# Sign of the weights by a rectifier's slope, and a weight decode laid over two steps, in an attention block with two MLPs

## The chip, the cores and the metric

The kernel runs on one core of one Trainium2 chip. The metric is the device time of one execution in microseconds; the time before is the median of three runs. A core has a matrix engine (TensorE; PE in the profile, with PEld for its loads of the stationary operand), a vector engine (VectorE; DVE), a scalar engine (ScalarE; ACT), a general engine (GpSimd; POOL) and a queue engine (SyncE; SP). Each works through its own list of instructions in order; semaphores hold an instruction until its inputs are there and its output buffer is free.

## The reference

```python
scores = softmax over states of x @ state^T / 8      # x: 8 batches, 8 heads, 512 x 64; state: 32 x 64
xread  = a @ state                                    # 8, 8, 512, 64
sread  = softmax over tokens of state @ x^T / 8, @ x  # 8, 8, 32, 64
x = concatenate(xread, sread), heads put side by side # 4352 tokens x 512

h = x @ w_in                                          # 512 -> 2048
x = (h * (1.0 / (1.0 + np.exp(-1.702 * h)))) @ w_out  # 2048 -> 512, first MLP
h = x @ w_in2
out = (h * np.cos(h)) @ w_out2                        # second MLP
```

The four weight matrices arrive as 64-bit floats, everything else as 32-bit floats.

## The kernel before

**Tiles and steps.** The tokens are nine tiles: the 512 read tokens of each batch (tiles 0 to 7) and the 256 state tokens of all batches together (tile 8, the tail). The hidden dimension of 2048 is cut into 16 chunks c of 128. A step is one (MLP m, tile t, chunk c). The first MLP takes its tiles in the order 0 to 6, 8, 7, the second 0 to 3, 8, 4 to 7. In each step TensorE computes `hidden` (the chunk's 128 columns of h into a PSUM tile ph), then `second` for the chunk two steps earlier (LAG = 2), which adds into four PSUM tiles py; ScalarE and VectorE make the activation in between (`gate` in the first MLP, `cosine` in the second). All of it stands in an order written out by hand.

**Two halves.** Each product is made of three matmuls: operands are split into a high half (a ScalarE copy into a rounded type) and a low half (a VectorE subtraction), and high x high, high x low and low x high are added. So a step of a full tile has 12 matmuls of 512 columns in `second`, and 12 in `hidden`, or 6 in tiles 1 to 7 of the first MLP: there the weights are multiplied by the batch's state beforehand (`sw_piece`: six matmuls of 256 columns, a ScalarE copy and a VectorE subtraction into a tile swo, and a write to DRAM from GpSimd's queue), and come back by `load_sw` as swt. The list `sw_steps` says in which step which of 16 pieces for each pair of batches is made. The attention of the next batch is spread over the steps in small parts too (`plan`).

**Decoding.** The 64-bit weights are fetched in units (128 x 1024 words each; 8 units of w_in and 8 of w_out for each MLP, `fetch_w`) and turned into two halves in five passes over 128 x 1024 elements:

- L117, ScalarE: the upper 32-bit word, read as a float and scaled, gives u (the exponent shifted into place);
- L122, ScalarE: the lower word, scaled to its top three bits, in place;
- L125, VectorE: u shifted left by three, OR the three bits;
- L128, VectorE: the sign bit of the upper word, OR u;
- L141, ScalarE: the high half; L143, VectorE: the low half.

L117 and L122 of one unit (`decode_begin`) stand in a step behind ScalarE's split of the gate's product (L367); L125 and L128 stand at that step's very end on VectorE, ahead of the next step's product (L377); L141 and L143 (`decode_end`) stand in the next step. The units of the first MLP are decoded in steps 0 to 13 of tile 0, w_out's and w_in's by turns; a w_out unit j is begun in step 2j and used by `second` in step 2j + 2. Those of the second MLP are decoded in the tail's steps 8, 11 and 14, in the odd steps of tile 7, and in steps 0, 2, 4, 6 and 8 of the second MLP's tile 0 (`at2`).

**Sums.** When a tile's 16 chunks are done, four `store`s copy py to SBUF (ScalarE, L444), and SP's queue writes them out. The copies use two buffers; the first MLP's tiles then come back by `load_y`. The buffers of the state pieces (swo) and of d in `cosine` are two others, with the tag "g".

Of the kernel before, what the change touches and what calls it, by code (L numbers as in the profile page):

```python
# [10 lines left out]
F32 = mybir.dt.float32  # L11
F32R = mybir.dt.float32r
I32 = mybir.dt.int32
U32 = mybir.dt.uint32
# [8 lines left out]
P = 128  # L23
# [18 lines left out]
def attention_two_mlps(  # L42
# [64 lines left out]
    def decode_begin(m, nm, j):  # L107

        raw = rawt.pop((m, nm, j))
        low, high = raw[:, :, 0], raw[:, :, 1]
        u = wtp.tile([P, UNIT], F32, name="u", tag="u")
        ui = u.bitcast(I32)

        nc.scalar.activation(out=u, in_=high.bitcast(F32), func=AF.Copy, scale=2.0**-112)  # L117
        wt[m, nm, j] = u
        begun.append((m, nm, j))

        def act():
            nc.scalar.activation(out=low, in_=low.bitcast(U32), func=AF.Copy, scale=TOP3)  # L122
# [9 lines left out]
        return act, bits  # L132

    def decode_end():

        if not begun:
            return lambda: None
        m, nm, j = begun.pop(0)
        u = wt[m, nm, j]
        w = wp.tile([P, 2, UNIT], F32R, name=f"w{nm}{m}_{j}", tag=f"w{nm}{j}")  # L140
        nc.scalar.activation(out=w[:, 0, :], in_=u, func=AF.Copy)  # L141
        wt[m, nm, j] = (w[:, 0, :], w[:, 1, :])
        return lambda: nc.vector.tensor_tensor(out=w[:, 1, :], in0=u, in1=w[:, 0, :].bitcast(F32), op=ALU.subtract)  # L143
# [227 lines left out]
    def gate(t, c, stores, unit):  # L371

        ph = ht.pop((0, t, c))
# [15 lines left out]

    def cosine(t, c, stores, before, unit, end):  # L390

        ph = ht[1, t, c]
# [4 lines left out]
        low_w = decode_end()  # L397
# [5 lines left out]
        act, bits = decode_begin(*unit) if unit else ((lambda: None),) * 2  # L403
# [4 lines left out]
        act()  # L408
        if low and not end:
            low()  # L410
        low_w()
# [3 lines left out]
        return bits  # L415
# [62 lines left out]
    def warm(n):  # L478
# [25 lines left out]
        ((0, 1), [(0, c) for c in (2, 4, 6, 7, 7, 10, 11, 11, 13, 13, 15)] + [(1, c) for c in (2, 3, 6, 8, 9)]),  # L504
        ((1, 10), [(1, c) for c in range(12, KF)] + [(2, c) for c in (2, 4, 5, 6, 9, 10, 11, 12, 14, 15)] + [(3, 0), (3, 2)]),
        ((3, 3), [(3, c) for c in (6, 9, 10, 12, 14, 15)] + [(4, c) for c in (2, 4, 6, 9, 10, 12, 14, 15)] + [(5, 0), (5, 2)]),
        ((5, 4), [(5, c) for c in (6, 9, 10, 12, 14, 15)] + [(6, c) for c in (2, 4, 5, 6, 9, 10, 11, 12, 14, 15)]),
# [34 lines left out]
    with tc.manual_schedule():  # L542
# [27 lines left out]
        act, bits = decode_begin(0, *seq[0])  # L570
        act()
# [3 lines left out]
        do("xread 0")  # L575
        bits()
        low_w = decode_end()
        do("sum_n 1", "turn_n 1", "split_x 0")
        low_w()
        do("xread 1")  # L580
        load_pair(0)
        act, bits = decode_begin(0, *seq[1])
        act()
        do("split_x 1")
        bits()
# [11 lines left out]
        at2 = [(0, B, c) for c in (8, 11, 14)] + [(0, B - 1, c) for c in range(1, KF, 2)] + [(1, 0, c) for c in range(0, 10, 2)]  # L597
# [98 lines left out]
```

## Time and profile before

| | |
|---|---|
| median of 3 runs | 1528.39 us (1526.99 to 1528.8) |
| profiled execution, its own time | 1530.31 us |
| its span | 1528.5 us |
| mean granted TensorE clock | 0.988 |
| TensorE busy | 1466.0 us (96%) |
| VectorE busy | 966.3 us (63%) |
| ScalarE busy | 644.1 us (42%) |
| GpSimd busy | 110.8 us (7%) |
| first slice of 38 us: TensorE busy | 7 tenths |
| slices 2 to 4: TensorE busy | 8, 7, 8 tenths; VectorE 8, 7, 7 |
| slices 20 and 21 (726 to 802 us): TensorE busy | 8, 8 tenths; VectorE 7, 7 |

Matmuls are pipelined and their ends are modelled, so a busy TensorE is not TensorE at its peak: what counts is how many matmuls start in a stretch. Idle time of an engine that no one waits for costs nothing. PEclk is the clock that the throttle granted, 1.00 or 0.50 of 2.4 GHz.

### The profile page before, as it was taken

Reading aid. Unit: us, or ns where it says so; the run is one execution under the profiler, and the core shown is the slowest. Engines: PE = TensorE matmul, PEld = TensorE weight load, DVE = VectorE, ACT = ScalarE, POOL = GpSimd, SP = SyncE. Lnnn points to the kernel's source line nnn. Section 1 sums busy time; section 2 is a strip of 40 time slices with the busy share of each in tenths; the row PEclk is TensorE's granted clock in tenths of the full one; section 3 lists DMA queues with packets and bytes.
Section 4 is the critical chain, followed back from the end, with each engine's and each line's share of the span. In section 5 each row is a group of like instructions: output and inputs, shape, how many; then the busy total and the mean of one; then the engine's idle time right before and its main releaser. Section 6 shows DMA issues by size and latency. Waiting matters only on the chain.

```text
span 1528.5 us, 19319 instructions
## 1 busy us (share of the span) xinstructions
PE 1466.0 (96%) x7306; PEld 1195.1 (78%) x7306; DVE 966.3 (63%) x1674; ACT 644.1 (42%) x1078; POOL 110.8 (7%) x155
## 2 busy tenths in 40 slices
PE   7878999999999999999889999999999999999998
PEld 4756777778887887897667888888888888888886
DVE  6877565546464646446778666666668666666665
ACT  4555334343434343345565433333344333333433
POOL 0011011110111000100001000010001010101000
PEclk8999999999999999999999999999999999999999
DMA  9544556564556343465320100101010001010000
GB/s 332 177 148 119 167 162 172 156 180 134 165 142 179 109 138 97 113 198 172 110 83 1 49 6 1 56 1 42 1 56 12 31 1 56 1 56 0 28 1 28
DMA packets 81340, 140.58 MB, mean 92 GB/s; under 512 B 11616, under 2 KB 38368, under 8 KB 81248
## 3 DMA queue, kind: packets, MB, share of 16 engines
q1 hardware_dynamic: 72000, 109.60, 22.5%
q0 software_dynamic: 8960, 29.37, 8.0%
q8 instruction: 57, 0.93, 0.3%
q10 hardware_dynamic: 288, 0.39, 0.1%
q14 instruction: 35, 0.29, 0.1%
HBM read 92.14 MB, written 47.19 MB: 91 GB/s over the span
## 4 chain that ended last, share of the span: by engine, by line
PE 74%; DVE 13%; ACT 7%; DMA 3%; issue 3%; SPq 0%; POOL 0%; ACTq 0%; DVEq 0%
PE py L438 38%; PE ph L360 23%; PE ph L353 8%; PE psS L170 2%; DVE u L125 2%; DVE u L128 2%; DVE t L377 1%; DMA yd<-o 1%; ACT u L117 1%; ACT gh L367 1%; PE psC L313 1%; ACT rawo L122 1%; PE psA L229 1%; DVE gl L369 1%; DVE wo L143 1%
## 5 line engine op out<-in xcount | busy, mean ns | idle before, releaser
L360 PE MATMUL ph<-xh,wi 128*128 128x512 f32 (+1 forms) x1280 | 406.2, 381 | 1.5 <-DVE t L377 1.5
L438 PE MATMUL py<-gh,wo 128*128 128x512 f32 (+1 forms) x1152 | 368.2, 382 | 17.0 <-ACT wo L141 9.6
L438 PE MATMUL py<-wo,gh 128*128 128x512 f32 x1088 | 337.6, 391 | 6.0 <-ACT o L444 5.3
L360 PEld LDWEIGHTS ph<-xh,wi 128*128 128x128 f32 x1280 | 238.7, 189 | 51.2 <-DVE t L377 1.9
L438 PEld LDWEIGHTS py<-gh,wo 128*128 128x128 f32 x1152 | 214.8, 190 | 65.6 <-ACT wo L141 12.1
L360 PE MATMUL ph<-xl,wi 128*128 128x512 f32 (+1 forms) x640 | 242.3, 381 | 0.0
L438 PEld LDWEIGHTS py<-wo,gh 128*128 128x128 f32 x1088 | 203.6, 189 | 48.9 <-ACT o L444 6.7
L438 PE MATMUL py<-gl,wo 128*128 128x512 f32 (+1 forms) x576 | 219.2, 381 | 0.0
L438 PE MATMUL py<-wo,gl 128*128 128x512 f32 x544 | 213.5, 392 | 4.8 <-DVE gl L369 4.7
L367 ACT ACTIVATE gh<-t 128x512 fp32r<-128x512 f32 (+1 forms) x144 | 87.6, 608 | 300.8 <-DVE t L377 185.9
L369 DVE TENSOR_TENSOR gl<-t,gh 128x512 fp32r<-128x512 f32 (+1 forms) x144 | 97.5, 677 | 166.7 <-ACT gh L367 166.7
L407 ACT ACTIVATE r<-r,half_pi 128x512 f32<-128x512 f32 (+1 forms) x144 | 101.0, 701 | 239.2 <-DVE r L406 239.2
L400 DVE TENSOR_SCALAR r<-r 128x512 f32<-128x512 f32 (+1 forms) x144 | 64.0, 444 | 176.2 <-ACT r L395 175.5
L353 PE MATMUL ph<-xh,swt 128*128 128x512 f32 x448 | 162.4, 403 | 7.5 <-DVE t L377 5.1
L395 ACT ACTIVATE r<-ph 128x512 f32<-128x512 f32 (+1 forms) x144 | 82.4, 573 | 169.1 <-PE ph L360 168.8
L377 DVE SCALAR_TENSOR_TENSOR t<-t,ph 128x512 f32<-128x512 f32 (+1 forms) x144 | 93.9, 652 | 84.3 <-ACT t L375 84.2
L360 PEld LDWEIGHTS ph<-xl,wi 128*128 128x128 f32 x640 | 121.2, 189 | 23.0
L438 PEld LDWEIGHTS py<-wo,gl 128*128 128x128 f32 x544 | 102.5, 188 | 30.5 <-DVE gl L369 9.4
L438 PEld LDWEIGHTS py<-gl,wo 128*128 128x128 f32 x576 | 109.6, 190 | 19.9
L419 DVE TENSOR_TENSOR r<-r,ph 128x512 f32<-128x512 f32 (+1 forms) x144 | 94.7, 657 | 45.0 <-ACT r L407 44.9
L375 ACT ACTIVATE t<-ph 128x512 f32<-128x512 f32 (+1 forms) x144 | 82.0, 569 | 83.3 <-PE ph L353 69.8
L353 PEld LDWEIGHTS ph<-xh,swt 128*128 128x128 f32 x448 | 85.4, 191 | 38.3 <-issue 14.7
(78 smaller groups left out, 1530.4 us busy)
## 6 DMA issues: line engine op xcount, KB each, us to landing
sd<-swo POOLq DMA_DIRECT2D x112, 256.0 KB, 3.8
swt<-sd SPq DMA_DIRECT2D x112, 256.0 KB, 4.2
rawi<-in_w_in SPq DMA_DIRECT2D x32, 512.0 KB, 5.8
rawo<-in_w_out SPq DMA_DIRECT2D x32, 512.0 KB, 5.7
xT_t<-in_xT SPq DMA_DIRECT2D x36, 256.0 KB, 4.0
xN_t<-in_xN SPq DMA_DIRECT2D x16, 512.0 KB, 3.9
yd<-o SPq DMA_DIRECT2D x32, 256.0 KB, 2.6
yraw<-yd SPq DMA_DIRECT2D x32, 256.0 KB, 4.3
```

The costliest lines, as they stand in the source:

```text
L125: nc.vector.scalar_tensor_tensor(out=ui, in0=ui, scalar=3, in1=low, op0=ALU.logical_shift_left, op1=ALU.bitwise_or)
L353: nc.tensor.matmul(ph, l, r, start=(g == 0 and i == 0), stop=(g == 1 and i == 2))
L360: nc.tensor.matmul(ph, w[:, f0:f0 + P], x, start=(w is wh and k == 0 and x is xk[0][0]), stop=(w is wl and k == KD - 1))
L367: nc.scalar.activation(out=gh, in_=g, func=AF.Copy)
L369: return lambda: nc.vector.tensor_tensor(out=gl, in0=g, in1=gh.bitcast(F32), op=ALU.subtract)
L375: nc.scalar.activation(out=t1, in_=ph, func=AF.Tanh, scale=0.5 * GATE)
L377: nc.vector.scalar_tensor_tensor(out=g, in0=t1, scalar=1.0, in1=ph, op0=ALU.add, op1=ALU.mult)
L395: nc.scalar.activation(out=r, in_=ph, func=AF.Copy, scale=1.0 / (2.0 * math.pi), bias=0.25)
L400: nc.vector.tensor_scalar(out=r, in0=r, scalar1=MAGIC, scalar2=MAGIC, op0=ALU.add, op1=ALU.subtract)
L407: nc.scalar.activation(out=r, in_=r, func=AF.Sin, bias=half_pi)
L419: nc.vector.tensor_tensor(out=r, in0=r, in1=ph, op=ALU.mult)
L438: nc.tensor.matmul(yt[k], l, r, start=(c == 0 and i == 0), stop=(c == KF - 1 and i == 2))
```

## The change

Four things change together.

1. `decode_begin`'s first pass is a parametric rectifier, `AF.Prelu`, with the same scale and a slope of -2^32 for negative inputs. A negative word's exponent thereby gets a bit that the later shift by three moves to the sign's place; the pass L128 is gone, and VectorE has one bit pass to a unit.
2. The parts of a unit are functions that `gate` and `cosine` place one by one: `top` (the rectifier) and `bottom` of a new unit, `bits`, `hi` and `lo` of the unit begun in the step before. `bits` stands behind the next step's product, no longer at the end of its own step; `lo` stands at the end of that next step.
3. Units of the second MLP are begun in the tail's steps 6, 9, 12 and 15, in the even steps of tile 7 from 2 on, and in steps 3, 5, 7, 10 and 12 of the second MLP's tile 0. `sw_steps` and the calls of `load_sw` are set anew: two more pieces in tile 0 (steps 5 and 12), the following pairs from (1, 7), (3, 0) and (5, 0).
4. In the first MLP the copies of sums 2 and 3 take the two buffers with the tag "g"; with the old two that is four.

```diff
-        nc.scalar.activation(out=u, in_=high.bitcast(F32), func=AF.Copy, scale=2.0**-112)
+        begun.append((m, nm, j, u, low))
+        def top():
+            nc.scalar.activation(out=u, in_=high.bitcast(F32), func=AF.Prelu, scale=2.0**-112, alpha=-(2.0**32))
+        def bottom():
             nc.scalar.activation(out=low, in_=low.bitcast(U32), func=AF.Copy, scale=TOP3)
...
-            nc.vector.scalar_tensor_tensor(
-                out=ui, in0=high, scalar=-(2**31), in1=ui, op0=ALU.bitwise_and, op1=ALU.bitwise_or
-            )
...
     def gate(t, c, stores, unit):
+        bits, hi, lo = decode_end()
+        top, bottom = decode_begin(*unit) if unit else (lambda: None,) * 2
...
         nc.vector.scalar_tensor_tensor(out=g, in0=t1, scalar=1.0, in1=ph, op0=ALU.add, op1=ALU.mult)
+        bits()
         for s in stores[:1]:
             s()
+        if not stores:
+            top()
         low = split_g(0, t, c, g)
-        low_w = decode_end()
-        act, bits = decode_begin(*unit) if unit else ((lambda: None),) * 2
-        act()
-        low()
-        low_w()
         for s in stores[1:]:
             s()
-        return bits
+        if stores:
+            top()
+        bottom()
+        hi()
+        low()
+        return lo
...
     def store(m, t, k):
-        o = op.tile([P, n if m == 0 else DM], F32, name="o", tag="o")
+        pool, tag = (ep, "g") if m == 0 and k >= 2 else (op, "o")
+        o = pool.tile([P, n if m == 0 else DM], F32, name="o", tag=tag)
...
-        at2 = [(0, B, c) for c in (8, 11, 14)] + [(0, B - 1, c) for c in range(1, KF, 2)] + [(1, 0, c) for c in range(0, 10, 2)]
+        at2 = [(0, B, c) for c in (6, 9, 12, 15)] + [(0, B - 1, c) for c in range(2, KF, 2)] + [(1, 0, c) for c in (3, 5, 7, 10, 12)]
```

`cosine` is changed likewise: `top` stands behind the first rounding pass, `bits`, `bottom` and `hi` behind the sine, `lo` at the step's end.

TensorE's list is the same in kind and number. Where the prediction speaks of the first tile, ScalarE's list before has this, step 3 and the start of step 4 (t is the gate's product, gh its high half, u a unit under way, rawi and rawo raw words, wo a decoded half; L293 and L244 are attention's):

```order
L375 ACTIVATE t_446<-ph 128x512
L367 ACTIVATE gh<-t_446 128x512
L141 ACTIVATE wo_1_452<-u 128x1024
L117 ACTIVATE u<-rawi_3_307 128x1024
L122 ACTIVATE rawi_3_307<-rawi_3_307 128x1024
L293 ACTIVATE a_462,s_463<-psA,b_405 128x512
L244 ACTIVATE T<-T 128x512
L375 ACTIVATE t_494<-ph 128x512
L367 ACTIVATE gh<-t_494 128x512
```

And now, the same steps:

```order
L382 ACTIVATE t_441<-ph 128x512
L120 ACTIVATE u<-rawi_3_304 128x1024
L372 ACTIVATE gh<-t_441 128x512
L123 ACTIVATE rawi_3_304<-rawi_3_304 128x1024
L142 ACTIVATE wo_1_450<-u 128x1024
L298 ACTIVATE a_456,s_457<-psA,b_400 128x512
L249 ACTIVATE T<-T 128x512
L382 ACTIVATE t_488<-ph 128x512
L120 ACTIVATE u<-rawo_2_334 128x1024
L372 ACTIVATE gh<-t_488 128x512
```

The top pass (L117, now L120) has moved ahead of the split of g, and the high half behind the bottom pass. VectorE's list before has, from the end of step 2 to the end of step 3 (L243 is attention's):

```order
L125 SCALAR_TENSOR_TENSOR u<-u,rawo_1_190 128x1024
L128 SCALAR_TENSOR_TENSOR u<-rawo_1_190,u 128x1024
L377 SCALAR_TENSOR_TENSOR t_446<-t_446,ph 128x512
L369 TENSOR_TENSOR gl<-t_446,gh 128x512
L143 TENSOR_TENSOR wo_1_452<-u,wo_1_452 128x1024
L243 TENSOR_TENSOR T<-T,m_401 128x512
L125 SCALAR_TENSOR_TENSOR u<-u,rawi_3_307 128x1024
L128 SCALAR_TENSOR_TENSOR u<-rawi_3_307,u 128x1024
```

And now, step 3 and the start of step 4:

```order
L384 SCALAR_TENSOR_TENSOR t_441<-t_441,ph 128x512
L136 SCALAR_TENSOR_TENSOR u<-u,rawo_1_190 128x1024
L374 TENSOR_TENSOR gl<-t_441,gh 128x512
L248 TENSOR_TENSOR T<-T,m_396 128x512
L146 TENSOR_TENSOR wo_1_450<-u,wo_1_450 128x1024
L384 SCALAR_TENSOR_TENSOR t_488<-t_488,ph 128x512
L136 SCALAR_TENSOR_TENSOR u<-u,rawi_3_304 128x1024
```

The bit pass of unit wo_1 stands behind the product of step 3 instead of ahead of it, and the unit's low half behind attention's pass. Where the prediction speaks of the second MLP's start, ScalarE's list before has, in steps 0 and 1 and the start of step 2 (r is the angle and then its sine, o a copied sum, py its PSUM tile):

```order
L117 ACTIVATE u<-rawo_3_6546 128x1024
L407 ACT_TABLE_LOAD
L407 ACTIVATE r<-r,half_pi 128x512
L122 ACTIVATE rawo_3_6546<-rawo_3_6546 128x1024
L395 ACTIVATE r<-ph 128x512
L367 ACTIVATE gh<-r 128x512
L141 ACTIVATE wo_3_6819<-u 128x1024
L444 ACTIVATE o<-py_6272 128x512
L444 ACTIVATE o<-py_6273 128x512
L444 ACTIVATE o<-py_6274 128x512
L407 ACTIVATE r<-r,half_pi 128x512
L444 ACTIVATE o<-py_6275 128x512
```

And now:

```order
L407 ACTIVATE r<-ph 128x512
L418 ACT_TABLE_LOAD
L418 ACTIVATE r<-r,half_pi 128x512
L407 ACTIVATE r<-ph 128x512
L372 ACTIVATE gh<-r 128x512
L457 ACTIVATE o<-py_6255 128x512
L457 ACTIVATE o<-py_6256 128x512
L457 ACTIVATE o<-py_6257 128x512
L418 ACTIVATE r<-r,half_pi 128x512
L457 ACTIVATE o<-py_6258 128x512
L407 ACTIVATE r<-ph 128x512
L372 ACTIVATE gh<-r 128x512
```

Between the two steps and the four copies of sums no weight pass is left. The table loads of the whole list are two before and two now, ahead of the first exponential and ahead of the first sine.

## Rows read from the trace of the kernel before

**Rows 1.** Table by stages: length, busy us (count) PE, PEld, DVE, ACT, POOL; clock, DMA.

```profile
45.00:144.40 99.40, 82.25 (x424) 63.55 (x423) 77.59 (x105) 56.16 (x79) 12.07 (x20) 0.98 0.41 122
691.00:759.00 68.00, 60.34 (x248) 47.83 (x246) 44.33 (x52) 37.61 (x54) 0.00 (x0) 0.95 0.44 144
759.00:834.00 75.00, 66.66 (x278) 52.91 (x279) 61.88 (x88) 44.68 (x62) 3.06 (x2) 0.95 0.17 56
1000.00:1100.00 100.00, 100.00 (x442) 82.72 (x442) 65.04 (x111) 38.30 (x65) 5.96 (x6) 1.00 0.05 16
```

**Rows 2.** Table by stages, at half clock (PEclk is the first figure after POOL).

```profile
212.80:216.20 3.40, 3.09 (x7) 2.48 (x8) 3.10 (x9) 0.10 (x1) 0.00 (x0) 0.51 1.05 355
694.00:700.80 6.80, 6.07 (x14) 4.78 (x15) 4.04 (x5) 3.40 (x7) 0.00 (x0) 0.50 0.46 129
776.00:782.70 6.70, 4.22 (x9) 2.89 (x10) 4.90 (x8) 4.63 (x9) 0.00 (x0) 0.50 0.31 114
```

**Rows 3.** Waits of TensorE, 42 to 145 us: total us, times, longest us.

```profile
PE py L438 <- ACT wo L141: 6.4, 5, 1.6
...
PE py L438 <- DVE wo L143: 2.6, 5, 0.5
```

**Rows 4.** Timeline of ScalarE, 90.5 to 98 us: start, us, line, out<-in, idle before.

```profile
90.85 0.63 ACT L367 ACTIVATE gh<-t 128x512 fp32r<-128x512 f32 x1 [3.42 <-DVE t L377]
91.39 1.04 ACT L141 ACTIVATE wi<-u 128x1024 fp32r<-128x1024 f32 x1
92.34 1.13 ACT L117 ACTIVATE u<-rawo 128x1024 f32<-128x1024 f32 x1
93.37 1.11 ACT L122 ACTIVATE rawo<-rawo 128x1024 int32<-128x1024 uint32 x1
...
97.69 0.63 ACT L367 ACTIVATE gh<-t 128x512 fp32r<-128x512 f32 x1 [2.73 <-DVE t L377]
```

**Rows 5.** Timeline of VectorE over the same step and the next.

```profile
94.51 1.22 DVE L125 SCALAR_TENSOR_TENSOR u<-u,rawo 128x1024 int32<-128x1024 int32 x1 [0.82 <-ACT rawo L122]
...
96.91 0.68 DVE L377 SCALAR_TENSOR_TENSOR t<-t,ph 128x512 f32<-128x512 f32 x1
...
99.29 1.23 DVE L143 TENSOR_TENSOR wo<-u,wo 128x1024 fp32r<-128x1024 f32 x1 [0.25 <-ACT wo L141]
```

**Rows 6.** Groups by line and shape, the state pieces' copies: busy us, mean ns, idle.

```profile
L175 DVE TENSOR_TENSOR swo<-psS,swo 128x512 fp32r<-128x512 f32 x64 | 43.5, 683 | 14.7 <-ACT swo L174 13.9 <-issue 0.3
...
L174 ACT ACTIVATE swo<-psS 128x512 fp32r<-128x512 f32 x64 | 37.4, 590 | 3.5 <-PE psS L170 1.3
```

**Rows 7.** Timeline of VectorE, step 9: first and last of twelve attention passes.

```profile
100.44 1.79 DVE L324 STREAM_TRANSPOSE xs<-psC 32x32 f32<-32x32 f32 x8
...
104.40 0.15 DVE L288 TENSOR_SCALAR b<-m 128x1 f32<-128x1 f32 x1
```

**Rows 8.** Timeline of ScalarE, last tile of the first MLP, two steps.

```profile
732.82 0.63 ACT L367 ACTIVATE gh<-t 128x512 fp32r<-128x512 f32 x1 [1.46 <-DVE t L377]
...
742.82 0.63 ACT L367 ACTIVATE gh<-t 128x512 fp32r<-128x512 f32 x1 [1.46 <-DVE t L377]
```

**Rows 9.** Waits of TensorE, 630 to 835 us.

```profile
PE py L438 <- ACT o L444: 9.5, 3, 5.3
PE ph L353 <- DVE t L377: 5.1, 5, 1.5
PE py L438 <- DVE gl L369: 2.8, 4, 1.0
```

**Rows 10.** Waits of TensorE, 160 to 300 us.

```profile
PE ph L353 <- DMA swt<-sd: 2.4, 1, 2.4
```

**Rows 11.** Timeline of TensorE in tile 6: start, us, line, out<-in, idle before.

```profile
608.66 0.50 PE L170 MATMUL psS<-wi,rhi 128*128 128x256 f32 x2 [1.73 <-DVE swo L175]
```

**Rows 12.** DMA issues of the page: KB each, median us to landing.

```profile
sd<-swo POOLq DMA_DIRECT2D x112, 256.0 KB, 3.8
```

**Rows 13.** Groups by line and shape: the table load.

```profile
L407 ACT ACT_TABLE_LOAD x1 | 1.3, 1283 | 0.0
```

More of the change, by code (lines that the diff above doesn't have):

```diff
@@ L114, in decode_begin, with decode_end @@
         u = wtp.tile([P, UNIT], F32, name="u", tag="u")
-        ui = u.bitcast(I32)
-        nc.scalar.activation(out=u, in_=high.bitcast(F32), func=AF.Copy, scale=2.0**-112)
[L118 to L122, printed above, removed]
+        begun.append((m, nm, j, u, low))
+        def top():
+            nc.scalar.activation(out=u, in_=high.bitcast(F32), func=AF.Prelu, scale=2.0**-112, alpha=-(2.0**32))
+        def bottom():
+            nc.scalar.activation(out=low, in_=low.bitcast(U32), func=AF.Copy, scale=TOP3)
+        return top, bottom
+    def decode_end():
+        if not begun:
+            return (lambda: None,) * 3
+        m, nm, j, u, low = begun.pop(0)
+        ui = u.bitcast(I32)
+        w = []
         def bits():
@@ L127, in bits, with hi, lo @@
             )
-            nc.vector.scalar_tensor_tensor(
-                out=ui, in0=high, scalar=-(2**31), in1=ui, op0=ALU.bitwise_and, op1=ALU.bitwise_or
-            )
[L132 to L143, printed above, removed]
+        def hi():
+            w.append(wp.tile([P, 2, UNIT], F32R, name=f"w{nm}{m}_{j}", tag=f"w{nm}{j}"))
+            nc.scalar.activation(out=w[0][:, 0, :], in_=u, func=AF.Copy)
+            wt[m, nm, j] = (w[0][:, 0, :], w[0][:, 1, :])
+        def lo():
+            nc.vector.tensor_tensor(out=w[0][:, 1, :], in0=u, in1=w[0][:, 0, :].bitcast(F32), op=ALU.subtract)
+        return bits, hi, lo
     xtile = {}
@@ L396, in cosine @@
         low = times(*before) if before else None
-        low_w = decode_end()
         if end:
@@ L402, in cosine @@
             s()
-        act, bits = decode_begin(*unit) if unit else ((lambda: None),) * 2
+        top()
         nc.vector.scalar_tensor_tensor(out=d, in0=r, scalar=-TWO_PI_HI, in1=ph, op0=ALU.mult, op1=ALU.add)
@@ L407, in cosine @@
         nc.scalar.activation(out=r, in_=r, func=AF.Sin, bias=half_pi)
-        act()
         if low and not end:
             low()
-        low_w()
+        bits()
+        bottom()
+        hi()
         for s in stores[-1:]:
@@ L414, in cosine @@
         ht[1, t, c] = (ph, r)
-        return bits
+        return lo
     def times(t, c):
@@ L569, in attention_two_mlps @@
         do("max_n 0", "exp_n 0")
-        act, bits = decode_begin(0, *seq[0])
-        act()
+        for part in decode_begin(0, *seq[0]):
+            part()
         do("max_n 1", "exp_n 1", "sum_n 0", "turn_n 0")
@@ L575, in attention_two_mlps @@
         do("xread 0")
+        bits, hi, lo = decode_end()
         bits()
-        low_w = decode_end()
+        hi()
         do("sum_n 1", "turn_n 1", "split_x 0")
-        low_w()
+        lo()
         do("xread 1")
         load_pair(0)
-        act, bits = decode_begin(0, *seq[1])
-        act()
+        for part in decode_begin(0, *seq[1]):
+            part()
         do("split_x 1")
-        bits()
         steps1 = [(0, t, c) for t in (*range(B - 1), B, B - 1) for c in range(KF)]
@@ L610, in attention_two_mlps @@
             if m == 0:
-                bits = gate(t, c, stores, unit)
+                lo = gate(t, c, stores, unit)
             else:
-                bits = cosine(t, c, stores, steps[i - 1][1:] if steps[i - 1][0] == 1 else None, unit, i + 1 == len(steps))
+                lo = cosine(t, c, stores, steps[i - 1][1:] if steps[i - 1][0] == 1 else None, unit, i + 1 == len(steps))
             if (m, t, c) in fetches:
@@ L623, in attention_two_mlps @@
                 sw_piece(*piece)
-            bits()
+            lo()
             if m == 0:
```

25 lines of the change are left out of this document (11 added, 14 removed).

## The prediction

> **What bounds the kernel now.** I read the busy shares first: TensorE is busy 96% of 1528.5 us, VectorE 63%, ScalarE 42%. So a faster pass on VectorE is worth nothing by itself, and the gain can only be time in which TensorE waits or runs at half clock. The table by stages says where that is. At its plain pace TensorE starts 442 matmuls of 512 columns in 100 us, 0.2262 us each [rows 1]. From 691 to 759 us it started 248 matmuls, worth 56.1 us, in 68.0; from 759 to 834 us 278, worth 62.9, in 75.0 [rows 1]. Those two stretches lose 11.9 and 12.1 us. They and the stretch from 45 to 144.4 us are the ones in which weights are decoded; elsewhere TensorE hardly waits.
>
> The waits name the cause. In the first tile TensorE waits for the high half of w_out (6.4 us in 5 waits) and then for its low half (2.6 us in 5) [rows 3]. In the second decoding it waits for copies of sums to leave PSUM (9.5 us in 3), for the gate's product (5.1 us in 5) and for low halves (2.8 us in 4) [rows 9].
>
> Behind the waits stands one closed chain through two engines. ScalarE's split of g (L367) comes at 90.85, then the three weight passes L141, L117, L122, and it idles until 97.69, waiting for VectorE's gate product L377 [rows 4]. VectorE's two bit passes L125 and L128 need the end of L122, and L377 stands behind them [rows 5]. Then the next L367 can go. Once around is 97.69 - 90.85 = 6.84 us, in a step with no attention and no state piece, whereas TensorE needs 24 x 0.2262 = 5.43. In the last tile of the first MLP the same chain takes two steps: 742.82 - 732.82 = 10.0 us [rows 8], whereas TensorE needs 36 x 0.2262 = 8.14.
>
> **The change part by part.** *The bit pass.* The second bit pass, 1.22 us [rows 5], goes 32 times, 39 us of VectorE. Its price on the path is not 39 us but what the chain gives.
>
> *The rectifier.* It replaces the Copy of L117 (1.13 us) [rows 4]; no extra pass. No row shows a Prelu. The nearest passes of 128x1024 take 1.04 to 1.13 us [rows 4]; I take 1.13 and allow 1.04 to 1.26 for the range, which is -1 to +1.6 us over the dozen passes on the chain of the first tile. The Trainium skill (ScalarE: Activation LUTs, What it computes and the timing under What ACT_TABLE_LOAD costs) says that every function streams one element a cycle and gives a fixed part of 186 ns with immediates; by it the pass would be an estimated 1.04 us, and the sum at most 1 us lower.
>
> *The interleaving.* In a decoding step the order on ScalarE becomes tanh, top of the new unit, split of g, bottom, high half of the old unit; on VectorE gate product, bit pass of the old unit, low half of g, attention's passes, low half of the old unit. The bit pass now reads what the step before made, so it waits for nothing, and the top pass fills ScalarE while VectorE makes the product. A new wait comes in: u has two buffers, so a top pass waits for the low-half pass of two units before, and the split of g stands behind that top pass. The new chain is low half, top, split of g, bottom, high half, low half. From row to row a ScalarE pass starts 0.1 us before the last one ends [rows 4], so that is 0.05 + 1.03 + 0.54 + 1.03 + 1.09 + 1.23 = 4.97 us; with a state piece, whose copies of 0.59 and 0.68 us [rows 6] stand before the low half, 6.1; with two, 6.8. TensorE needs 5.43, 6.15 and 6.87 (a piece is 6 matmuls of half width, about 0.72). So TensorE is last, by little, in every step without much attention on VectorE.
>
> *First tile (45 to 144.4 us).* Start: the high half of the second w_in unit is now made after the split of g, not before the tile, and I lay the start 0.6 us later; the half clock there stays. From 45.7 us TensorE has 12 x 5.43 = 65.2, eleven pieces 7.9 and attention's matmuls about 3.6 (estimate from their columns), 76.7 us. I laid steps 2 to 14 out with the durations of rows 4 to 7. The high halves of w_out come in time; the low halves, asked for by the third matmul, are late in five steps. The clearest is step 9: attention's twelve passes run from 100.44 to 104.55 [rows 7], 4.1 us, ahead of the low half, so VectorE has 0.68 + 1.22 + 0.7 (the low half of g, taken like the product) + 4.1 + 1.23 = 7.9 us against TensorE's 5.43, and TensorE waits some 2.45. The five are 0.75, 0.65, 2.45, 2.85, 0.95, in all 7.65. That ends the stretch at 45.7 + 76.7 + 7.65 = 130.0 instead of 144.4: **14.4 us**. Two more of the state pieces lie in this tile than before, and so two fewer later, where TensorE has no other wait: **1.4**. Bounds: if all low halves come in time, 22; if each of the five is a further 1 us late, 9.4.
>
> *State products.* The last pieces of the first pair move from steps 8 and 9 of tile 1 to 5 and 12 of tile 0, and the loads of chunks 12 to 15 from step 10 on to step 7 on. The wait of 2.4 us for them goes [rows 10], and with it the half clock of 3.4 us that came behind it [rows 2], worth 1.7: **4.1**. SP's queue is moved too: chunks 8 to 11 are asked for at steps 0 to 3; their buffers are free then and their pieces stored, so nothing queues behind them. In tile 6 a piece behind a transpose made TensorE wait 1.73 us [rows 11]; that step has none now: **1.7** (0 if it waits elsewhere).
>
> *Tail tile and last tile.* The two steps of the chain become, with the split of y, 7.8 us against TensorE's 8.14: TensorE is last, and the 11.9 us go, except some 0.5 where the tail's sums still wait behind a split of g: **11.4** (8.5 to 11.9). Half clock from 694.0 to 700.8 us [rows 2], 3.4 us, is in it. In the tail, the first copy wait and two waits for the product, some 3.4 us of rows 9: **3.4** (1.6 to 4.5).
>
> *Start of the second MLP (759 to 834 us).* No unit is begun in its first three steps, and the four sums have four buffers, so the copies of the old tile no longer stand behind weight passes and output DMAs; the 5.3 us wait [rows 9] and the half clock behind it (6.7 us, worth 3.35) [rows 2] go. VectorE is busy 61.9 of 75 us here [rows 1]; without some five bit passes it still has about 85% of the shorter stretch, so half of the waits for low halves may stay, 1.5: 12.1 - 1.5 = **10.6** (7.5 to 12.1).
>
> *Sum.* 14.4 + 1.4 + 4.1 + 1.7 + 11.4 + 3.4 + 10.6 = 47.0. The profiled execution took 1530.3 us (its span 1528.5); that makes 1483.3. It lay 1.9 above the median of the runs, 1528.4, so I forecast **1481 us**. From there to the end TensorE has no wait that the change touches.
>
> **Rivals.** *1. The low half stays last and the clock falls.* Waits of 2.4 to 5.3 us in this trace came before every half-clock stretch behind the start [rows 2, 9, 10]; the two largest that I leave in the first tile, 2.45 and 2.85, are of that size. If the low halves are 1 us later each (-5), two or three stretches at half clock follow (1.7 each, -5) and the second MLP keeps its waits (-3), the result is some 1494. For it: VectorE's sum in steps 9 and 11. Against: the handovers that I laid out have 0.05 us each.
>
> *2. The shared buffers wait.* Sums 2 and 3 now take the buffers of the state pieces, whose DMA lands after 3.8 us [rows 12]. If each of seven tile changes holds ScalarE that long, less about 1.4 us of slack, TensorE waits 2.4 us seven times, with half clock (1.7) behind each: 29 us back, 1510. Against: the pieces were written a step of 5 us or more before.
>
> *3. Slower: the rectifier needs another function table.* If Prelu lay in another table than Tanh and Sin, each of 32 top passes would need a load before and after it, 2 x 1.28 us [rows 13]. In the first tile every step's chain of about 7.0 us would be 9.55: 12 x 2.57 = 31 us back, and beyond; the last tile's two-step chain 10.4 instead of 7.8, above the old 10.0 (9 back); the second MLP some 6 to 9, the tail 3 to 4: 1481 + 31 + 9 + 8 + 4 = 1533, slower than before. It decides from about 2.4 us extra per pass. Against: the changed program has the same two table loads as the old one, at the same places. The Trainium skill (ScalarE: Activation LUTs, Table sets) puts a switch at some 2.66 us with its drain; by that this rival would be near 1580, and rows 13 show only the 1.28.
>
> **How the numbers follow.** Forecast as laid out, 1471 to 1490: 0.70. Below 1471, the first tile without waits: 0.05. Rival 1, 1490 to 1503: 0.17. Rival 2: 0.05. Rival 3: 0.03. The range of 8 in 10 is 1470 to 1500: the bounds of the first tile (+5, -8), of the second MLP (+3, -1.5) and the last tile (+3) do not all fall on one side, and rival 1's nearer part is in it. A measurement of this kernel tells about 0.2% from no change, 3 us: faster 0.96, within 0.2% 0.01, slower 0.03.
>
> **What would show it.** Right: Prelu passes of 1.04 to 1.26 us, only two table loads; no wait for the high half of w_out after step 2, waits for low halves near 7 us in all in tile 0, its step 15 begun near 130 us; no half clock at the change to the last tile and to the second MLP; steps of 4.07 us in the last tile of the first MLP; no wait of TensorE for chunks 12 to 15 in tile 1. Wrong: ScalarE's split of g waiting for a top pass that waits for a low half in most steps; TensorE waiting for state pieces or sums at tile changes; table loads around the rectifier.

## The result, and the profile after

The changed kernel takes **1491.86 us**, median of 4 runs (1490.73 to 1493.11), against 1527.69 us of the kernel before in the same series: 0.9765 of the time, 95% interval 0.9749 to 0.9782. The profiled execution took 1492.88 us, its span 1491.1 us. So 37.4 us of span went, where the prediction had 47.0; the time lies in the range, 11 us above the forecast and 2 us from rival 1.

The first line of the page's busy times, after:

```profile
PE 1455.3 (98%) x7306; PEld 1192.2 (80%) x7306; DVE 927.7 (62%) x1642; ACT 646.7 (43%) x1078; POOL 111.4 (7%) x155
```

VectorE lost the 32 second bit passes, 38.6 us of its 966.3. Below is the span cut at the starts of `hidden`'s first matmul of a tile, read from the timelines of TensorE (us of each stage). The columns besides before and after are kernels of the experiments; the last version is the kernel of 1469.64 us. Four of the experiments' kernels give every engine the same order of work in the first tile, and yet their first stage takes 127.1, 128.1, 128.3 and 129.5 us, the longer the more of it ran at half clock; differences of that size in the first row, and of 1 or 2 us in the last, need not be effects of an edit.

| stage | forecast saving | before | after | saved | rectifier alone | order alone | all but the order | last version |
|---|---|---|---|---|---|---|---|---|
| start and first tile | 14.4 | 147.9 | 139.7 | 8.2 | 129.3 | 150.2 | 131.5 | 129.5 |
| tile 1 | 4.1 | 88.7 | 87.7 | 1.0 | 87.0 | 88.3 | 87.6 | 82.8 |
| tiles 2 to 6 | 1.4 + 1.7 | 392.7 | 387.3 | 5.4 | 392.4 | 387.3 | 387.3 | 387.6 |
| tail | 3.4 | 53.1 | 50.0 | 3.1 | 51.8 | 50.0 | 50.0 | 50.1 |
| tile 7 | 11.4 | 76.9 | 63.4 | 13.6 | 67.0 | 67.3 | 64.3 | 63.4 |
| second MLP, 19 steps | 10.6 | 115.4 | 108.3 | 7.1 | 107.4 | 116.4 | 103.4 | 103.4 |
| the rest | 0 | 653.9 | 654.8 | -0.9 | 654.3 | 654.3 | 653.1 | 651.9 |

The tail came out 0.3 us below its forecast and tile 7 2.2 above it. The first tile, tile 1 and the second MLP fell short. The table by stages of the changed kernel (columns as in rows 1) has in its first line the stretch that answers to 45.00:144.40 of before, then the first four steps of the second MLP and the twelve behind them, then three pieces around stretches at half clock, each window begun 0.3 us ahead of the fall:

```profile
40.40:135.85 95.45, 84.24 (x436) 67.08 (x435) 65.03 (x95) 59.00 (x80) 14.49 (x24) 0.95 0.55 158
727.79:749.55 21.76, 21.76 (x97) 18.02 (x97) 13.87 (x23) 11.96 (x18) 0.00 (x0) 1.00 0.56 193
749.55:819.16 69.61, 66.87 (x289) 53.69 (x289) 55.36 (x83) 38.21 (x54) 6.23 (x4) 1.00 0.00 1
94.20:97.70 3.50, 3.50 (x11) 2.68 (x10) 1.26 (x2) 0.70 (x1) 0.00 (x0) 0.55 0.04 16
111.30:118.10 6.80, 5.92 (x17) 4.85 (x18) 3.15 (x4) 2.42 (x3) 1.89 (x4) 0.52 0.63 157
213.70:217.10 3.40, 2.81 (x10) 2.52 (x11) 2.45 (x5) 2.12 (x4) 1.20 (x2) 0.54 0.40 77
```

In the first line the stretch is about 4 us shorter than the 99.40 of before, where the working had it end 14.4 earlier, and its clock is lower than before (0.95 against 0.98 in [rows 1]): two pieces of it, 3.4 us from 94.5 and 6.8 us from 111.6, ran at the 1.2 GHz level. At the change to the second MLP TensorE is busy throughout (21.76 of 21.76; before, the change and the steps behind it together had 66.66 of 75.00 [rows 1]), and no half clock is left there or at tile 7 [rows 2]. In the steps behind, 289 matmuls are worth 65.4 us and take 69.6.

TensorE's waits (total us, times, longest us), first from 30 to 145 us, then from 150 to 300 and from 560 to 850:

```profile
PE py L450 <- DVE wo L146: 12.7, 7, 3.4
PE py L450 <- ACT wo L142: 1.6, 1, 1.6
```

```profile
PE psS L175 <- DVE swo L180: 4.2, 2, 2.4
```

```profile
PE py L450 <- DVE gl L374: 2.5, 3, 1.3
PE ph L365 <- POOL xtail L476: 0.4, 2, 0.2
PE py L450 <- ACT o L457: 0.3, 1, 0.3
```

The wait for the high half, 9.6 us before from 30 us on (6.4 of it from 42 us on [rows 3]), fell to 1.6; the wait for the low half, 2.6 us before, rose to 12.7. In the second decode the 9.5 us for sums and the 5.1 us for the gate's product [rows 9] are gone, and the low half of g remains.

What the low half stands behind is seen on VectorE in steps 9 and 10 (timeline of VectorE, then of ScalarE and of TensorE: start, us, line, output and input, in brackets the idle time before and what ended it):

```profile
85.14 0.69 DVE L384 SCALAR_TENSOR_TENSOR t<-t,ph 128x512 f32<-128x512 f32 x1 [1.52 <-ACT t L382]
85.75 1.22 DVE L136 SCALAR_TENSOR_TENSOR u<-u,rawo 128x1024 int32<-128x1024 int32 x1
87.89 0.69 DVE L374 TENSOR_TENSOR gl<-t,gh 128x512 fp32r<-128x512 f32 x1 [0.93 <-ACT gh L372]
88.50 1.79 DVE L329 STREAM_TRANSPOSE xs<-psC 32x32 f32<-32x32 f32 x8
...
92.44 0.15 DVE L293 TENSOR_SCALAR b<-m 128x1 f32<-128x1 f32 x1
92.51 1.22 DVE L146 TENSOR_TENSOR wo<-u,wo 128x1024 fp32r<-128x1024 f32 x1
```

```profile
87.23 0.63 ACT L372 ACTIVATE gh<-t 128x512 fp32r<-128x512 f32 x1 [1.10 <-PE py L450]
87.77 1.12 ACT L123 ACTIVATE rawi<-rawi 128x1024 int32<-128x1024 uint32 x1
88.79 1.05 ACT L142 ACTIVATE wo<-u 128x1024 fp32r<-128x1024 f32 x1
```

```profile
93.78 0.73 PE L450 MATMUL py<-gh,wo 128*128 128x512 f32 x2 [3.16 <-DVE wo L146]
```

From the product at 85.14 to the end of the low half at 93.73 VectorE needs 8.6 us. 4.0 of them are attention's passes, issued ahead of the low half; 0.93 is a wait of the low half of g for ScalarE's split, which itself waited 1.10 for TensorE to be done with the g of two steps before. The high half had been ready at 89.84. TensorE then stood 3.16 us, and the clock fell at 94.5.

The Trainium skill (PSUM — Partial Sum Buffer, Engine vs sequencer instructions) calls the queues of ScalarE and VectorE strictly first in, first out; for VectorE these rows agree: the high half was there 2.7 us before it came to the low half.

### The profile page after: what moved, and what is told of

Its sections match the earlier page's. It is cut to its first block, busy times and chain, and to the rows that moved or that the text cites. A ratio compares the mean times of both kernels' runs of the same rounds, so it can differ in the third digit from the quotient of the medians.

```text
span 1491.1 us, 19321 instructions
## 1 busy us (share of the span) xinstructions
PE 1455.3 (98%) x7306; PEld 1192.2 (80%) x7306; DVE 927.7 (62%) x1642; ACT 646.7 (43%) x1078; POOL 111.4 (7%) x155
## 4 chain that ended last, share of the span: by engine, by line
PE 81%; DVE 7%; ACT 3%; DMA 1%; issue 1%; POOL 0%; ACTq 0%; DVEq 0%
PE py L450 43%; PE ph L365 23%; PE ph L358 10%; PE psS L175 2%; PE psC L318 1%; DMA out<-o 1%; PE psA L234 1%; DVE r L411 1%; DVE r L416 1%; DVE d L415 1%; DVE gl L374 1%; DVE wo L146 1%; ACT gh L372 0%; ACT o L457 0%; DVE u L136 0%
## 5 line engine op out<-in xcount | busy, mean ns | idle before, releaser
L450 PE MATMUL py<-gh,wo 128*128 128x512 f32 (+1 forms) x1152 | 367.0, 382 | 14.7 <-DVE wo L146 12.7
L372 ACT ACTIVATE gh<-t 128x512 fp32r<-128x512 f32 (+1 forms) x144 | 87.5, 608 | 256.8 <-PE py L450 160.3
```

The source lines that it names most:

```text
L372: nc.scalar.activation(out=gh, in_=g, func=AF.Copy)
L450: nc.tensor.matmul(yt[k], l, r, start=(c == 0 and i == 0), stop=(c == KF - 1 and i == 2))
```

## Experiments

Two theories were to be told apart. A: the low half is late because the chain closes through TensorE (the split of g waits for the second product of two steps before, and the rest stands behind it). B: it is late because VectorE has attention's passes ahead of it. All kernels are edits of the changed kernel unless the text says otherwise. In the expectations a wait is the excess of the time from one matmul's start to the next over the usual spacing; in the rows it is the idle time of the profile.

**Which part saves the time: the rectifier alone.** The kernel before, with these two edits:

```diff
-        nc.scalar.activation(out=u, in_=high.bitcast(F32), func=AF.Copy, scale=2.0**-112)
+        nc.scalar.activation(out=u, in_=high.bitcast(F32), func=AF.Prelu, scale=2.0**-112, alpha=-(2.0**32))
...
-            nc.vector.scalar_tensor_tensor(
-                out=ui, in0=high, scalar=-(2**31), in1=ui, op0=ALU.bitwise_and, op1=ALU.bitwise_or
-            )
```

> The kernel before, with the rectifier in place of the Copy and one bit pass instead of two, in the old order, with the old buffers and the old places of pieces and units. If the chain of the prediction is right (6.84 us a step in the first tile, 10.0 us for two steps in the last), taking 1.22 us out of it gives 5.6 and 8.8 us against TensorE's 5.43 to 6.15 and 8.14: 8 to 14 us of the first tile, 7 to 8.5 of the last, 2 to 5 at the start of the second MLP: 1501 to 1511. If the passes on VectorE were not on the path and the order alone does it: 1522 to 1528.

Measured: 1491.94 us, ratio 0.9763 (0.9748 to 0.9777). The same as the whole change. Both stories fall: the passes were on the path, and taking 1.22 us out of each step gave more than the 17 to 27 us that the chain had room for. Part of the rest is clock: in the first stage of this trace 3.4 us ran at half clock, against 17.1 before. Its waits of TensorE from 30 to 145 us, and then from 560 to 850:

```profile
PE py L435 <- ACT wo L138: 3.2, 2, 1.9
PE py L435 <- DVE wo L140: 2.1, 4, 0.5
```

```profile
PE py L435 <- ACT o L441: 6.4, 5, 2.0
```

In the old order the low half stands ahead of attention's passes and is never late by more than 0.5 us: the first tile with its start takes 129.3 us, 10 less than in the changed kernel. The sums wait again, and tile 7 takes 67.0.

**The order without the rectifier.** The changed kernel with the Copy in the top pass, and both bit passes, one behind the other, in the decode's end.

> The changed kernel with the Copy in place of the rectifier and both bit passes, one behind the other, as the decode's end: the interleaving, buffers and places of the change without the rectifier. If the new order breaks the old chain by itself, as the prediction laid it out (a chain of 4.97 us that holds no bit pass), the second bit pass costs next to nothing: 1490 to 1496. If VectorE's queue ahead of the low half is what counts, each low half in the first tile is 1.2 us later (6 waits, +7, and more half clock behind them, +2 to +5) and the second MLP's five units add 3 to 6: 1503 to 1515.

Measured: 1514.55 us, ratio 0.9913 (0.9892 to 0.9935), at the top of the second answer. TensorE's waits from 30 to 150 us, and from 700 to 850:

```profile
PE py L453 <- DVE wo L149: 15.6, 7, 4.0
PE py L453 <- ACT wo L145: 2.5, 2, 2.0
```

```profile
PE py L453 <- DVE gl L377: 7.2, 6, 2.0
```

The waits for low halves are 2.9 us more than with one bit pass, and from 30 us to the tile's end 20.5 us ran at half clock against 13.7. A pass that the laid-out chain did not even contain costs 22.7 us (1514.55 against 1491.86).

**All but the order.** The kernel before with the rectifier, and with all the rest of the change (four buffers for sums; the new places of pieces, loads and units), but the old order of the gate and of the second MLP's step.

> The kernel before with the rectifier and one bit pass, and with all that the change does besides the order of the decode: four buffers for sums, the new places of state pieces, of loads and of the second decode's units. The gate and the second MLP's step keep the old order (split of g, low half of it, low half of the weights, then attention). If the new order only costs, the first tile takes the 103.7 us that the rectifier alone showed instead of 113.6, and tiles 6, tail and 7 come to the changed kernel's 76.7, 50.0 and 63.4: 1478 to 1483. If the new order is what brings TensorE to its pace in tile 7 (the old chain of two steps is 8.8 us against 8.14), tile 7 stays near 67, and the second MLP's start, with units in steps 10 and 12, near 108: 1484 to 1489.

Measured: 1478.65 us, ratio 0.9684 (0.9671 to 0.9697). First answer: the new order only costs, here 13.2 us. The first tile takes 131.5 us against 139.7, and the start of the second MLP 103.4 against 108.3; only tile 7 is 1.0 longer.

**The low half first.**

```diff
                 lo = gate(t, c, stores, unit)
+                lo()
...
-            lo()
+            if m:
+                lo()
```

> The changed kernel, with one edit: in the gate's steps the low half of the old unit is issued on VectorE ahead of the attention and state passes of the step, not behind them. Theory A (loop through TensorE): the split of g has two buffers, so it waits until TensorE has ended the second product of two steps before; the low half comes split 0.54 + bottom 1.03 + high half 1.09 + low half 1.23 = 3.9 us behind that, while TensorE asks for it 14 matmuls = 3.2 us later (0.72 more per state piece). So with attention out of the way about 0.7 us of wait stays in every second step without a piece, some 2 to 4 us in all instead of 12.1, and no half clock behind it: 1476 to 1481. Theory B (VectorE's order alone): the low half is late only because attention's passes stand ahead of it; all waits for low halves in the first tile go: 1472 to 1476.

Measured: 1479.69 us, ratio 0.9682 (0.9665 to 0.9698): the time of theory A, but of the low half's waits only 1.6 us stay, which is nearer to theory B. TensorE's waits from 30 to 145 us, then VectorE in the same step as above:

```profile
PE py L450 <- ACT wo L142: 2.7, 2, 1.6
PE psS L175 <- DVE swo L180: 1.6, 1, 1.6
PE py L450 <- DVE wo L146: 1.6, 3, 0.5
```

```profile
81.39 0.69 DVE L384 SCALAR_TENSOR_TENSOR t<-t,ph 128x512 f32<-128x512 f32 x1 [1.52 <-ACT t L382]
82.00 1.22 DVE L136 SCALAR_TENSOR_TENSOR u<-u,rawo 128x1024 int32<-128x1024 int32 x1
84.15 0.69 DVE L374 TENSOR_TENSOR gl<-t,gh 128x512 fp32r<-128x512 f32 x1 [0.93 <-ACT gh L372]
86.12 1.23 DVE L146 TENSOR_TENSOR wo<-u,wo 128x1024 fp32r<-128x1024 f32 x1 [1.28 <-ACT wo L142]
87.26 1.79 DVE L329 STREAM_TRANSPOSE xs<-psC 32x32 f32<-32x32 f32 x8
```

VectorE now stands idle for 1.28 us to wait for the high half, and it pays: the low half ends 5.96 us behind the product's start, not 8.59, and 11 of the 12.7 us of waits go. No half clock is left in the stretch that answers to the first line of the table by stages:

```profile
38.80:124.20 85.40, 79.89 (x435) 63.88 (x434) 66.13 (x97) 58.60 (x80) 14.49 (x24) 1.00 0.60 177
```

**The high half ahead of the bottom pass.** `bottom()` and `hi()` in the gate change places.

> The changed kernel, with one edit: in the gate's steps ScalarE makes the high half of the old unit ahead of the bottom pass of the new one, not behind it. Theory A (loop through TensorE): the chain from the end of the second product to the low half falls from 3.9 to 2.9 us, below the 3.2 us after which TensorE asks for it; the small waits (0.70, 1.53, 1.71, 1.18) go or fall below 0.7, the two behind attention's passes (3.34 and 3.61) fall by about 1 each: 12.1 becomes 5 to 6, and 1482 to 1487. Theory B (VectorE's order alone): the low half waits for VectorE and not for the high half, so nothing moves: 1490 to 1493.

Measured: 1490.74 us, ratio 0.9759 (0.9744 to 0.9774), as theory B has it. The waits stay:

```profile
PE py L450 <- DVE wo L146: 13.9, 7, 3.4
```

Theory A's chain of ScalarE passes is not what the low half waits for; VectorE's queue is.

**Both old halves ahead of the split of g.** In the gate `hi()` stands ahead of the split of g, and `lo()` ahead of the low half of g.

> The changed kernel, with one edit: in the gate's steps both halves of the old unit come ahead of the split of g, the high half on ScalarE before it and the low half on VectorE before the low half of g and all attention passes, so that neither stands behind an instruction that waits for TensorE. Theories A and B both expect no wait for low halves above 0.3 us in the first tile from step 4 on and no half clock at 94 and 111 us: 1472 to 1477. If waits of over 1 us stay, a third cause (the top pass waiting for the second buffer of u, or attention's passes now late) is at work, and 1480 or more.

Measured: 1481.27 us, ratio 0.9693 (0.9679 to 0.9708). Low halves are late by 1.1 us in 2 waits, nearly as both theories said, but the time is 4 us above them, in the last answer's range. In this trace a transpose of attention waits for a state piece's copy (2.0 us, 1.3 with the low half first), and 3.4 us at half clock follow, worth 1.7; the rest of the 4 us is not explained.

**The low half of g behind that of the weights.** In the gate `low()` is called behind `lo()`, both still behind attention's passes.

> The changed kernel, with one edit: in the gate's steps VectorE makes the low half of g behind the low half of the old unit, so that no instruction ahead of the low half waits, through the split of g, for TensorE's second product; attention's passes stay ahead of it. If that wait (0.93 us in the step before 89.95, which the prediction left out) is the difference between the 2.45 that I laid out and the 3.34 measured, the waits for low halves fall by 0.5 to 1 each, 12.1 becomes 7 to 9, and one or both half-clock stretches go: 1483 to 1488. If attention's passes alone set it: 1490 to 1493.

Measured: 1483.75 us, ratio 0.9712 (0.9695 to 0.973): the time of the first answer, for another reason. Waits of VectorE from 40 to 145 us, of the changed kernel, then of this one:

```profile
DVE gl L374 <- ACT gh L372: 17.2, 11, 3.7
DVE swo L180 <- ACT swo L179: 7.1, 5, 2.4
```

```profile
DVE swo L180 <- ACT swo L179: 15.0, 7, 4.0
DVE gl L374 <- ACT gh L372: 2.0, 1, 2.0
```

The wait for the split of g fell from 17.2 us to 2.0, and that for the state pieces' copies, which stand behind the same split on ScalarE, rose from 7.1 to 15.0. TensorE's waits for low halves fell from 12.7 to 11.6 only. The two profiled spans lie 11.6 us apart, more than the medians: 3.8 of that came in the first tile (6.8 us less at half clock) and 6.8 in tiles 1 to 6, most of it in tile 1, where waits for state pieces went. So this run did not open the loop of theory A; it moved the wait.

**The sums in two buffers again.** `store` takes its buffers from `op` alone.

> The changed kernel with the sums of the first MLP in two buffers again, as before, and all else as changed. If the four buffers took the copy waits away, they come back at the changes of tiles with a decode (tile 6 to the tail 3 to 4 us, tail to tile 7 and tile 7 to the second MLP 1 to 4 each): 1497 to 1503. If the place of the top pass behind the copies did it, nothing moves: 1490 to 1493.

Measured: 1496.22 us, ratio 0.9798 (0.978 to 0.9817); between the two answers. The tail takes 51.8 instead of 50.0 us and tile 7 64.3 instead of 63.4, with a wait that the changed kernel has at 0.3:

```profile
PE py L450 <- ACT o L456: 2.5, 3, 1.6
```

So the buffers are worth 2.8 us by these two stages, 4.4 by the medians (the two profiled spans differ by 0.6 only: in this execution no half clock followed the wait in tile 1, and that tile is 1.4 shorter). Tile 6 did not move (76.7): its gain belongs to the moved pieces.

**Two pieces out of the way of transposes,** on top of the low half first:

```diff
-        ((1, 7), [(1, c) for c in (8, 9, 12, 13, 14, 15)] + [(2, c) for c in (2, 4, 5, 6, 9, 10, 11, 12, 14, 15)]),
+        ((1, 7), [(1, c) for c in (8, 9, 12, 14, 15)] + [(2, c) for c in (0, 2, 4, 5, 6, 9, 10, 12, 13, 14, 15)]),
```

> The kernel with the low half first, and two state pieces moved out of the steps in which a transpose takes the same PSUM buffers: from step 13 of tile 1 to step 0 of tile 2, and from step 11 of tile 2 to step 13. If these two waits (2.63 and 1.95 us) and the half clock behind the first (3.4 us, worth 1.7) come from the neighbourhood of piece and transpose, they go: 1472 to 1475. If the waits only move to the pieces' new places: 1477 to 1481.

Measured: 1472.64 us, ratio 0.9644 (0.9628 to 0.966), as the first answer. TensorE's waits for state pieces between 150 and 300 us fell from 4.2 us to

```profile
PE psS L175 <- DVE swo L180: 0.3, 1, 0.3
```

and tile 1 from 87.5 to 82.9 us: 4.6 of the 7.1 us. The rest lies in stretches that the edit does not touch.

**The bit pass ahead of the cosine,** on top of that:

```diff
         top()
+        bits()
+        hi()
...
             low()
-        bits()
         bottom()
-        hi()
```

> The kernel with the low half first and two pieces moved, with one more edit, in the second MLP's steps: bit pass and high half of the old unit are issued ahead of the cosine's reduction, not behind the sine. In the trace of the kernel with the low half first VectorE stands 1.19 us before each low half there, waiting for the high half, and the next product and with it the low half of r come late. If that idle time is the cause of the 4.1 us that TensorE loses between 755 and 812 us, 3 to 4 of it go: 1468 to 1470. If VectorE's sum in a decoding step (6.8 us against 5.43) is the cause, or the sine behind the bit pass comes late in its turn: 1471 to 1475.

Measured: **1469.64 us**, ratio 0.9622 (0.9609 to 0.9635), as the first answer: faster than both kernels. VectorE in a decoding step of the second MLP, changed kernel, then this one:

```profile
767.86 1.22 DVE L136 SCALAR_TENSOR_TENSOR u<-u,rawo 128x1024 int32<-128x1024 int32 x1
770.27 1.23 DVE L146 TENSOR_TENSOR wo<-u,wo 128x1024 fp32r<-128x1024 f32 x1 [1.19 <-ACT wo L142]
771.41 0.68 DVE L431 TENSOR_TENSOR r<-r,ph 128x512 f32<-128x512 f32 x1
```

```profile
761.33 1.22 DVE L136 SCALAR_TENSOR_TENSOR u<-u,rawo 128x1024 int32<-128x1024 int32 x1
...
764.25 0.68 DVE L374 TENSOR_TENSOR gl<-r,gh 128x512 fp32r<-128x512 f32 x1
764.85 1.22 DVE L146 TENSOR_TENSOR wo<-u,wo 128x1024 fp32r<-128x1024 f32 x1
```

With four passes between bit pass and low half there is no idle time, and steps 4 to 15 of the tile take 65.3 us, TensorE's own pace.

**The old order with the two pieces moved.**

> The kernel in the old order with the rectifier and the side changes, and the two state pieces moved as in the kernel with the low half first. If the new order, with its low half put first and the second MLP's bit pass early, is worth something, this one stays behind that kernel's 1469.6: the two waits of 2.63 and 1.95 us and one half clock go, 1478.65 - 6 = 1472 to 1474, with the first tile some 3 us longer and tile 7 one. If the order is worth nothing, 1468 to 1471.

Measured: 1475.81 us, ratio 0.9659 (0.9645 to 0.9674). It gained 2.8 us where 5 to 6 were expected: tile 1 gave its 4.5, and 1 to 2 us went elsewhere, in stretches that the edit does not touch, which no run explains. So the interleaving, with the low half first and the bit pass early, gains 6.2 us by the medians (1475.81 against 1469.64). By the stages some 3 to 5 us of that belong to it: tile 7 takes 63.4 instead of 64.3 and the first stage 129.5 instead of 131.6 (127.1 to 129.5 over the four kernels with the low half first); 2 us lie in the last row of the table, where no weight is decoded. As the change has it, the interleaving costs 13.

**The rectifier's own price.**

> The kernel with the low half first, two pieces moved and the early bit pass, with the Copy in place of the rectifier in the top pass, and still one bit pass: the signs of the weights are left out, everything else is the same. If the rectifier costs what its rows say (1.12 to 1.18 us against 1.10 to 1.14 of the Copy), the time is the same within 1 us: 1468.5 to 1470.5. If its pass is on the path, 32 x 0.04 = 1.3 us faster at most: 1468. If the function cost a change of tables that the rows hide, 1455 or less.

Measured: 1468.93 us (1468.91 to 1469.05), ratio 0.9617 (0.9603 to 0.9631), against 1469.64 (1467.95 to 1470.87): no difference. The passes by group, with the rectifier in the changed kernel, then with the Copy in this one (busy us, mean ns, idle time before):

```profile
L120 ACT ACTIVATE u<-rawi 128x1024 f32<-128x1024 f32 x16 | 18.3, 1144 | 6.1 <-DVE wi L146 4.6 <-issue 1.5
L120 ACT ACTIVATE u<-rawo 128x1024 f32<-128x1024 f32 x16 | 18.2, 1138 | 11.1 <-DVE wo L146 5.8 <-issue 4.5 <-DVE wi L146 0.8
```

```profile
L120 ACT ACTIVATE u<-rawi 128x1024 f32<-128x1024 f32 x16 | 18.2, 1136 | 1.0 <-DVE wi L146 0.8 <-DMA rawi<-in_w_in 0.2
L120 ACT ACTIVATE u<-rawo 128x1024 f32<-128x1024 f32 x16 | 18.1, 1130 | 0.9 <-DVE wo L146 0.9
```

## Why the prediction was right, and where not

**The time and the range** held, because the range was stretched to rival 1, and rival 1 is what happened: the low half stayed last in VectorE's queue, the clock fell twice in the first tile, and the second MLP kept its waits for the low half of g. It had said 1494; the kernel takes 1491.9. Rival 1's three terms (5 for the waits, 5 for the clock, 3 for the second MLP) came out as 2.9, 5.1 and 3.5. That the whole ends within 2 us of it is in part luck: the start (5.0 us better than laid out), tile 7 (2.2) and tiles 2 to 6 (2.3) outweigh by about 2 us what tile 1 (3.1), TensorE's own work in the first tile (3.2) and the last row (0.9) cost.

**The rectifier.** 1.13 us was taken, 1.14 measured, with two table loads as before: rival 3 is out. Its sum was too small besides: a chain of 10.4 us against TensorE's 8.14 gives back 8 x 2.26 = 18 us in the last tile, not 9. By the Trainium skill (ScalarE: Activation LUTs, What ACT_TABLE_LOAD costs) a pass was an estimated 1.04; the rows have 1.14, and they decide. Rival 2 is out too: at the tile changes of the decode TensorE waits 0.3 us for a sum.

**The first tile, 14.4 us forecast, 8.2 measured.** Three steps of the working failed, not all in one direction.
- The start was laid 0.6 us later, with its half clock kept; step 3's first matmul came 4.4 us earlier (38.0 against 42.4 us). The second bit pass had also stood ahead of attention's passes before the first step, and TensorE waited for their result. Its longest wait before step 0, before and after:

```profile
PE psX L275 <- DVE aT L261: 3.8, 1, 3.8
PE psX L280 <- DVE aT L266: 2.2, 1, 2.2
```

  With both bit passes in the new order this wait is 3.8 us again, 6.8 us at half clock come with it from 17.2, and step 2 began at 30.1 us, as in the kernel before (29.4); in the twelve kernels with one pass it began between 25.6 and 27.9. The clock has a large part in that: from 18.2 and from 35.3 us the kernel before ran 6.8 us each at half clock, the changed one only 3.4, from 33.1. In the other kernels with one pass the first of these pieces is 3.4 us long or missing, and it differs between kernels with the same order up to there, so how the 4.4 us divide is not shown.
- The five waits for low halves were laid out at 7.65 us; they came to 10.5 (12.7 with the two ahead of them), with 10.2 us at half clock behind the two largest, worth 5.1. For step 9 VectorE's sum of 7.9 us against a measured 8.6 shows what the lay-out left out: the low half of g waits 0.93 us for ScalarE's split, and the split, with two buffers, 1.10 for TensorE. The chain that I laid out closes through VectorE and ScalarE only. By these rows a late low half can delay the second product, that a later split, that the low half of g, and behind it stand attention's passes and the next low half: it would close through TensorE as well. That this makes 7.65 into 10.5 is argued, not shown: the run that was to open this loop took only 1.1 us off TensorE's waits and moved VectorE's wait to other instructions. What is shown is the order on VectorE: with the low half ahead of attention's passes 11 of the 12.7 us go, and with the high half made earlier none. The sign of being wrong that the prediction names, a top pass waiting for a low half, is there too: 10.4 us of ScalarE's time in seven waits of this tile, 3.22 of it at 93.76, just behind the late low half.
- TensorE's own work was laid out at 76.7 us; with the low half first TensorE is busy 79.9 in that stretch, and it takes 85.4. So the bound of 22 us for "all low halves in time" was too good: there TensorE waits for high halves, state pieces and a transpose's input in turn.

**"TensorE is last, by little, in every step without much attention on VectorE"** is right for tile 7 (63.4 us, 13.6 saved for 11.4) and nearly so for the tail (3.1 for 3.4). But the reason given, the new chain, was not needed: with the old order and all else tile 7 takes 64.3.

**Tile 1, 4.1 forecast, 1.0 measured.** The wait for chunks 12 to 15 went, with its half clock [rows 2, 10]. A wait of 2.4 us took its place, for a state piece that now stands right behind a transpose (TensorE's rows at 211.23 and 214.29), with 3.4 us at half clock from 214.0. It was the rule by which I had given tile 6 its 1.7 us [rows 11], and I did not apply it to tile 1. Tiles 2 to 6 gave 5.4 for 3.1; 3.8 of that is tile 6.

**The start of the second MLP, 10.6 forecast, 7.1 measured.** The wait for sums and its half clock went, as laid out. The allowance of 1.5 us for VectorE was too small: 4.2 are lost behind step 4. VectorE's load was not the cause, as I had it, but 1.19 us of idle time ahead of each low half; the version without it loses nothing. The rest of the span is 0.9 us longer than before. It varies from 651.9 to 654.8 over all these kernels, and by 1.3 between two whose second MLP is the same, so it lies within that scatter.

**What the gain is due to** was wrong as the text told it. It gave the bit pass no price on the path and let the interleaving break the chains. The runs show the reverse: the rectifier alone brings all 36 us, the side changes another 13 (1491.94 to 1478.65), and the order takes those 13 back. The parts do not simply add: with the new order and the side changes already in, the second bit pass is worth 22.7 us, not 36.

## What to carry to other kernels

When a pass is split off and issued later, look at what its queue holds ahead of it: work that is needed only later (here attention's passes, 4 us) must stand behind work that TensorE asks for now, even if the engine idles a little for it. When laying out a chain, follow each buffer's release too, until the chain either ends or closes, through the bounding engine as well. When comparing two traces stage by stage, read the granted clock of each stage first. And when several edits come together, price each alone: two of these made the kernel 49 us faster, the third gave 13 back, and the sum hid it.

## What was not expected of the hardware

The rectifier runs at the Copy's pace (1138 to 1144 ns against 1130 to 1136 for 128x1024), with the slope for negative inputs applied in the same pass. The granted clock fell to its lower level, for 3.4 or 6.8 us, during or just behind waits of TensorE of 3.16, 3.45 and 2.43 us in the middle of dense work of the changed kernel (ended at 93.8, 112.2 and 214.3 us). Shorter waits came before a fall in other runs: 1.33 us with the rectifier alone (ended at 44.6, half clock from 46.6) and 1.54 us in the kernel of 1469.64 us (ended at 32.2, half clock from 34.4). And a wait of 2.42 us did not, with the sums in two buffers (ended at 214.8). In the profiled execution of the 1472.64 us kernel, whose longest wait behind the start is 1.6 us, no stretch at half clock lies ahead of its last matmul; the kernel of 1469.64 us has the same order of work at its start and has two, of 3.4 us each. So what such a wait costs in clock differs from one execution to the next.
